# An attention and mixture-of-experts kernel: PSUM tiles in a named ring, value loads on SyncE's queue

## The chip, the cores and the metric

The kernel runs on one core of a Trainium2 chip. A core has TensorE (PE; its weight loads are listed as PEld), VectorE (DVE), ScalarE (ACT), GpSimd (POOL) and SyncE (SP), and 16 DMA engines that serve the transfers which SP, ACT and POOL issue. The metric is the device time of one execution in microseconds, median of several runs.

## The reference

Attention over 4 batches of 12 heads, 448 positions and head size 64, with the scores capped by `cap * tanh(scores / cap)`; its output, 1792 rows of 768, goes through a mixture of 8 experts, of which each row takes the one with the highest gate logit:

```python
scores = cap * np.tanh(scale * np.matmul(q, k.transpose(0, 1, 3, 2)) / cap)
attn = np.exp(scores - np.max(scores, axis=-1, keepdims=True))
attn = attn / (np.sum(attn, axis=-1, keepdims=True) + 1e-09)
x = np.matmul(attn, v)                                  # (4, 12, 448, 64) -> (1792, 768)
e_idx = np.argmax(x @ w_gate, axis=1)
h = np.maximum(x[mask] @ w1[e], 0.0)                    # for each expert e, mask = e_idx == e
out[mask] = gate_w[mask, None] * eom[mask, e, None] * (h @ w2[e])
```

`gate_w` is the softmax weight of the chosen expert, `eom` a sigmoid of `x @ w_output_gate`. Inputs and output are float32.

## The kernel before, in words

The work has two halves. In the attention half a loop (line 908) goes over 24 units; unit u is a pair of heads of one batch (six pairs per batch). The expert half takes the rows, sorted by expert, through `w1` and `w2` in blocks; its matmuls (line 1006) read weights that ACT and DVE have split into a high and a low part.

One turn of the loop for unit u does, in the order in which each engine gets its instructions:

- PE makes three score tiles `s` (`qk`, line 344; each holds both heads for 128 keys) and a fourth, half as large (`s3`, line 349). ACT takes the tanh of each out of PSUM into `pt` (line 351), then the exponential of the whole of `pt` in one instruction (line 353). `pt` has two buffers.
- PE multiplies unit u-1's `pt` with its values into `u` (`pv`, line 361, 16 matmuls), which ACT or DVE copies to `ut` (`u_evac`, lines 380 and 382).
- DVE turns K and Q of unit u+2 (`t_k`, `t_q`: a transpose at line 294 into `tk`, then a high and a low part). POOL adds up `pt` over keys (`presum`, lines 370 to 375), which PE sums across partitions every second unit (line 394).
- `slot` calls (line 897) put in the work that ends the batch before: PE turns `ut` into rows (`trow`, line 535), DVE scales them (`xr`, line 539) and SP's queue writes them to `xs` (line 544); gate products (`tg`, line 441; `pg`, line 456), ranks (`trk`) and POOL's table writes (line 526) belong to it too. In the last batch but one these steps also choose the experts' blocks, and the first weights are fetched.

The order on each engine is the order of the code. All score tiles, `u`, and the tiles `trow`, `tg`, `pg`, `trk` and `trec` of the batches' ends but the last's come from one pool, `ps_s`, of three PSUM buffers of two banks each (`scores` and `half`, lines 316 and 319). A tile can be written when the tile that had its buffer before has been read. Which of the three free buffers a tile gets is the pool's choice while the program is built, and is fixed in the program.

DMAs: K (`load_k`, six per unit into `kk`, four buffers) and Q (`load_q`, four for two units, `lq`) are issued on SP's queue, four units ahead of the loop, after the first scores; the values (`load_v`, four per unit, `vv`, three buffers) on ACT's queue right behind the exponential, for the next unit. The `xs` writes stand on SP's queue too. A queue issues its DMAs in its order. Each DMA of SP and ACT gets one of eight completion counters (DMAHW0 to DMAHW7), which go round over both queues, and is issued only when the DMA that had the counter before it has landed.

Of the kernel before, what the change touches and what calls it, by code (L numbers as in the profile page):

```python
# [9 lines left out]
F32 = mybir.dt.float32  # L10
# [12 lines left out]
def tile_kernel(ctx: ExitStack, tc, q, k, v, cap, w_gate, w_ogate, w1, w2, out):  # L23
    nc = tc.nc
# [46 lines left out]
    utp = rou.enter_context(tc.tile_pool(name="utp", bufs=8, side="right"))  # L71
    xrp = rou.enter_context(tc.tile_pool(name="xrp", bufs=3, side="right"))
    rtp = rou.enter_context(tc.tile_pool(name="rtp", bufs=1, side="right"))
# [6 lines left out]
    ptp = att.enter_context(tc.tile_pool(name="ptp", bufs=2))  # L80
    ps_s = att.enter_context(tc.tile_pool(name="ps_s", bufs=3, space=PSUM))

# [228 lines left out]
    def turn_next(n):  # L311
        for f, u in turns[:n]:
            f(u)
        del turns[:n]

    def scores(name):
        return ps_s.tile([128, 2, 512], F32, tag="s", name=name)

# [3 lines left out]
    def prep_first():  # L322
        pk = tbank([128, SK + 128], "tk0")
        for c in range(NK + 1):
            nc.tensor.transpose(pk[:, c * 128:(c + 1) * 128], k0[:, c].rearrange("p j d -> p (j d)"), ident)
        pq = ps_s.tile([128, 2, 512], F32, tag="s", name="tq0")[:, 0, 0:S]
        for c in range(NCH):
            nc.tensor.transpose(pq[:, c * CP:(c + 1) * CP], q0[:, c].rearrange("p j d -> p (j d)"), ident[0:CP, 0:CP])
        pl[0] = planes_of(0, pk, "K", SK + 128) + planes_of(0, pq, "Q", S)
        scales()  # L330
# [67 lines left out]
    rt = {}  # L398
    moe = []
    sh = [CP, NCH, E]  # L400

# [4 lines left out]
    def end_of_batch(b):  # L406
# [130 lines left out]
        def row_out(p):  # L537
            x = xrp.tile([CP, NCH, 128], F32, tag="xr", name="xr")
            nc.vector.tensor_tensor(  # L539
                out=x.rearrange("p c (j d) -> p c j d", j=2), in0=rt["trow"].rearrange("p c (j d) -> p c j d", j=2),  # L540
                in1=rec[b][:, :, 2 * p:2 * p + 2].unsqueeze(3).to_broadcast([CP, NCH, 2, D]), op=ALU.mult)
            for j in range(2):
                h = p + j * NP
                (nc.gpsimd if b == B - 1 else nc.sync).dma_start(
                    out=xs[b * S:(b + 1) * S, D * h:D * h + D].rearrange("(c p) m -> p c m", c=NCH),
                    in_=x[:, :, D * j:D * j + D])
# [361 lines left out]
    for u in range(NU):  # L908
# [11 lines left out]
        qk(u, NK)  # L920
        load_v(u + 1, nc.scalar)
        slot(u, "h")
# [360 lines left out]
```

## Time and profile before

| | us |
|---|---|
| median of 3 runs | 575.87 (574.64 to 578.27) |
| profiled execution | 577.18 |
| its span, first to last instruction | 575.3 |
| PE busy | 514.5 |
| ACT busy | 373.3 |
| DVE busy | 371.7 |
| POOL busy | 304.6 |

The profile is of one execution; times in it count from the first instruction. Busy time is an average over halves with different limits, so each stage is read by itself. An entry such as "0.97 <-PE s L344" says that the engine stood idle for 0.97 us before the instruction, and that PE's work on `s` at line 344 ended the wait. The granted clock is the share of 2.4 GHz that PE was given.

### The profile page before, as it was taken

The page shows a single profiled execution, that of the slowest core. Times are in us where ns is not written, and L with a number is a line of the kernel's source. Part 1 is how long each engine was busy: PE and PEld are TensorE (multiplying, and loading weights), DVE is VectorE, ACT ScalarE, POOL GpSimd, SP SyncE. Part 2 cuts the span into 40 slices and gives each one's busy share as a digit, 9 for nine tenths or more (in the row PEclk, how much of TensorE's full clock was granted, in tenths as well). Part 3 has the DMA queues.
Part 4 walks back from the last instruction along what each step waited for, and adds up shares of the span by engine and source line. Part 5 has one row for each costly group of instructions (what it writes and reads, how often), then busy time and mean ns, then how long its engine had stood idle before and what let it go on. Part 6 is the DMA issues. An engine that isn't in the chain of part 4 may idle for free. (4 is left out here: it accounts for less than half of the span.)

```text
span 575.3 us, 10035 instructions
## 1 busy us (share of the span) xinstructions
PE 514.5 (89%) x3053; PEld 348.9 (61%) x3053; DVE 371.7 (65%) x629; ACT 373.3 (65%) x425; POOL 304.6 (53%) x347
## 2 busy tenths in 40 slices
PE   7798678987678788896999999999999999999994
PEld 5444333533333245433789899789788886767692
DVE  4545656574254577776999998697576775646460
ACT  6688646777545657565375898687677776656561
POOL 8868744764954476644570576731474804362001
PEclk9799978999877997798999999999999999999998
DMA  6655443554551645368860992442956968985001
GB/s 144 95 88 92 74 72 64 93 92 84 58 89 28 117 81 93 65 169 287 277 228 1 339 398 67 159 152 85 380 202 214 389 268 338 411 281 238 8 29 45
DMA packets 157772, 91.93 MB, mean 160 GB/s; under 512 B 140418, under 2 KB 140554, under 8 KB 157712
## 3 DMA queue, kind: packets, MB, share of 16 engines
q1 hardware_dynamic: 125632, 52.96, 35.1%
q0 software_dynamic: 8832, 32.74, 15.2%
q10 hardware_dynamic: 23248, 5.53, 4.6%
q8 instruction: 26, 0.43, 0.3%
q14 instruction: 34, 0.28, 0.2%
HBM read 123.68 MB, written 12.04 MB: 236 GB/s over the span
## 5 line engine op out<-in xcount | busy, mean ns | idle before, releaser
L985 DVE TENSOR_TENSOR wr<-raw,wr 128x768 fp32r<-128x768 f32 (+1 forms) x167 | 171.6, 1068 | 66.2 <-ACT wr L984 64.0
L984 ACT ACTIVATE wr<-raw 128x768 fp32r<-128x768 f32 (+1 forms) x167 | 150.4, 936 | 33.2 <-DMA raw<-in_moe_w_dram 13.0
L351 ACT ACTIVATE pt<-s,icap 128x896 f32<-128x896 f32 x96 | 84.6, 912 | 71.2 <-PE s L344 31.1
L361 PE MATMUL u<-pt,vv 128*64 128x448 f32 x384 | 88.0, 606 | 9.4 <-ACT pt L351 9.3
L1006 PE MATMUL py<-wr,hh 128*128 128x384 f32 x352 | 77.3, 340 | 0.0
L370 POOL TENSOR_TENSOR pa<-pt 128x896 f32<-128x896 f32 x22 | 46.1, 2095 | 57.4 <-ACT pt L353 48.8
L1006 PE MATMUL php<-wr,xh 128*128 128x512 f32 x264 | 74.7, 404 | 0.0
L353 ACT ACTIVATE pt<-pt,capc 128x3136 f32<-128x3136 f32 x24 | 69.8, 2910 | 0.8
L1075 POOL DMA_INDIRECT out_dram<-yo,ti x13 | 20.6, 1585 | 84.6 <-ACT yo L1073 61.1
L361 PEld LDWEIGHTS u<-pt,vv 128*64 128x64 f32 x384 | 28.3, 153 | 60.8 <-issue 41.7
L1006 PEld LDWEIGHTS py<-wr,hh 128*128 128x128 f32 x352 | 61.2, 188 | 4.0 <-issue 3.7
L1006 PEld LDWEIGHTS php<-wr,xh 128*128 128x128 f32 x264 | 47.5, 188 | 12.2 <-issue 2.1
L344 PE MATMUL s<-QH,KH 64*128 64x448 f32 x144 | 32.8, 450 | 23.9 <-ACT pt L351 16.8
L375 POOL TENSOR_TENSOR pb<-pb,pt 64x448 f32<-64x448 f32 x44 | 49.9, 1135 | 3.4
L371 POOL TENSOR_TENSOR pb<-pa,pt 128x896 f32<-128x896 f32 x22 | 46.2, 2099 | 4.4 <-PE sm L394 2.8
L294 DVE STREAM_TRANSPOSE tk<-kk 128x512 f32<-128x512 f32 x23 | 16.7, 725 | 47.2 <-DMA kk<-in_k_dram 45.4
L1006 PE MATMUL py<-wr,hl 128*128 128x384 f32 x176 | 44.8, 335 | 0.0
L344 PEld LDWEIGHTS s<-QH,KH 64*128 64x128 f32 x144 | 14.6, 197 | 47.3 <-ACT pt L351 23.9
L1006 PE MATMUL php<-wr,xl 128*128 128x512 f32 x132 | 41.5, 395 | 0.0
L1122 POOL DMA_DIRECT2D rh<-in_moe_w_dram x42 | 23.2, 555 | 23.0 <-DVE wr L985 13.6
L1006 PEld LDWEIGHTS py<-wr,hl 128*128 128x128 f32 x176 | 31.8, 188 | 0.0
L539 DVE TENSOR_TENSOR xr<-trow,rec 112x512 f32<-112x512 f32 x24 | 16.2, 687 | 20.9 <-DMA xs<-xr 10.7
(247 smaller groups left out, 828.5 us busy)
## 6 DMA issues: line engine op xcount, KB each, us to landing
raw<-in_moe_w_dram SPq DMA_DIRECT2D x78, 512.0 KB
raw<-in_moe_w_dram SPq DMA_DIRECT2D x104, 384.0 KB
rh<-in_moe_w_dram POOLq DMA_DIRECT2D x18, 512.0 KB
rh<-in_moe_w_dram POOLq DMA_DIRECT2D x24, 384.0 KB
lq<-in_q_dram SPq DMA_DIRECT2D x44, 112.0 KB
vv<-in_v_dram ACTq DMA_DIRECT2D x46, 96.0 KB
xs<-xr SPq DMA_DIRECT2D x36, 112.0 KB
kk<-in_k_dram SPq DMA_DIRECT2D x46, 56.0 KB
```

Source lines behind the costliest of these rows:

```text
L344: nc.tensor.matmul(ps[:, j, 0:S], lhsT=x[h, sl], rhs=y[h], start=(i == 0), stop=(i == 2))
L351: nc.scalar.activation(out=pt[u][:, 2 * s:2 * s + n], in_=ps, func=ACTF.Tanh, scale=icap)
L353: nc.scalar.activation(out=pt[u], in_=pt[u], func=ACTF.Exp, scale=capc)
L361: nc.tensor.matmul(ups[u][64 * j:64 * j + 64], lhsT=V[:, c, j, :], rhs=P[:, 2 * c + (j if c < NK else 0)], start=(c == 0), stop=(c == NK))
L370: eng.tensor_tensor(out=a, in0=P[:, 0:2], in1=P[:, 2:4], op=ALU.add)
L371: eng.tensor_tensor(out=s1[u], in0=a, in1=P[:, 4:6], op=ALU.add)
L375: eng.tensor_tensor(out=s1[u][h, j], in0=s1[u][h, j], in1=P[h, 2 * NK], op=ALU.add)
L984: nc.scalar.activation(out=t[:, 0, 0:F], in_=raw, func=ACTF.Copy)
L985: nc.vector.tensor_tensor(out=t[:, 1, 0:F], in0=raw, in1=t[:, 0, 0:F].bitcast(F32), op=ALU.subtract)
L1006: nc.tensor.matmul(ps[g][:, 0:n], lhsT=st[:, c], rhs=w[:, z, g * n:(g + 1) * n], start=(c == 0 and st is hi and z == 0), stop=(c == (KD, K ...
L1075: nc.gpsimd.indirect_dma_start(out=out, out_offset=bass.IndirectOffsetOnAxis(ap=ti, axis=0), in_=y, in_offset=None, bounds_check=NT - 1, o ...
L1122: nc.gpsimd.dma_start(out=d, in_=rows_of(src, e, w, c), **kw)
```

## The change

Three edits. `scores` takes its buffers by name, `s0`, `s1`, `s2`, in strict turn, each name with one buffer; the three buffers stay three. The row buffers `xr` get names in the same way. `load_v` is called with SP's queue in place of ACT's, at the same place in the code (the first call, before the loop, was on SP already).

```diff
--- before.py
+++ after.py
@@ -69,7 +69,7 @@
     wp1 = ctx.enter_context(tc.tile_pool(name="wp1", bufs=1))
     rou = ExitStack()
     utp = rou.enter_context(tc.tile_pool(name="utp", bufs=8, side="right"))
-    xrp = rou.enter_context(tc.tile_pool(name="xrp", bufs=3, side="right"))
+    xrp = rou.enter_context(tc.tile_pool(name="xrp", bufs=1, side="right"))
     rtp = rou.enter_context(tc.tile_pool(name="rtp", bufs=1, side="right"))
     smp = rou.enter_context(tc.tile_pool(name="smp", bufs=2, side="right"))
     ps_t = ctx.enter_context(tc.tile_pool(name="ps_t", bufs=1, space=PSUM))
@@ -78,7 +78,7 @@
     plp = att.enter_context(tc.tile_pool(name="plp", bufs=3))
     ldp = att.enter_context(tc.tile_pool(name="ldp", bufs=2))
     ptp = att.enter_context(tc.tile_pool(name="ptp", bufs=2))
-    ps_s = att.enter_context(tc.tile_pool(name="ps_s", bufs=3, space=PSUM))
+    ps_s = att.enter_context(tc.tile_pool(name="ps_s", bufs=1, space=PSUM))
 
     tpools = [ps_t]
 
@@ -313,8 +313,11 @@
             f(u)
         del turns[:n]
 
+    ring = [0]
+
     def scores(name):
-        return ps_s.tile([128, 2, 512], F32, tag="s", name=name)
+        ring[0] += 1
+        return ps_s.tile([128, 2, 512], F32, tag=f"s{ring[0] % 3}", name=name)
 
     def half(name):
         return scores(name)[:, 0]
@@ -323,7 +326,7 @@
         pk = tbank([128, SK + 128], "tk0")
         for c in range(NK + 1):
             nc.tensor.transpose(pk[:, c * 128:(c + 1) * 128], k0[:, c].rearrange("p j d -> p (j d)"), ident)
-        pq = ps_s.tile([128, 2, 512], F32, tag="s", name="tq0")[:, 0, 0:S]
+        pq = scores("tq0")[:, 0, 0:S]
         for c in range(NCH):
             nc.tensor.transpose(pq[:, c * CP:(c + 1) * CP], q0[:, c].rearrange("p j d -> p (j d)"), ident[0:CP, 0:CP])
         pl[0] = planes_of(0, pk, "K", SK + 128) + planes_of(0, pq, "Q", S)
@@ -397,6 +400,7 @@
 
     rt = {}
     moe = []
+    nrow = [0]
     sh = [CP, NCH, E]
 
     def T(nm, shape=None, dt=F32):
@@ -535,7 +539,8 @@
                 nc.tensor.transpose(ps[:, c, :], ut[b * NP + p][:, c * CP:(c + 1) * CP], ident)
 
         def row_out(p):
-            x = xrp.tile([CP, NCH, 128], F32, tag="xr", name="xr")
+            nrow[0] += 1
+            x = xrp.tile([CP, NCH, 128], F32, tag=f"xr{nrow[0] % 3}", name="xr")
             nc.vector.tensor_tensor(
                 out=x.rearrange("p c (j d) -> p c j d", j=2), in0=rt["trow"].rearrange("p c (j d) -> p c j d", j=2),
                 in1=rec[b][:, :, 2 * p:2 * p + 2].unsqueeze(3).to_broadcast([CP, NCH, 2, D]), op=ALU.mult)
@@ -918,7 +923,7 @@
         slot(u, "f")
         slot(u, "g")
         qk(u, NK)
-        load_v(u + 1, nc.scalar)
+        load_v(u + 1, nc.sync)
         slot(u, "h")
         if u > 0:
             for c in range(NK + 1):
```

No instruction of PE, DVE or POOL moves. What each engine waits for changes with the buffers. The buffers in the two built programs (A, B, C in the order of their addresses), for some turns of the loop; the line stands between what comes before the fourth score tile's products with `u` and what comes after:

```
turn   before                          changed
 7     sB sB sB s3B | uB tgA           sA sB sC s3A | uB tgC
 8     sC sC sC trecC s3A | uB         sA sB sC trecA s3B | uC
11     sB sA sC trowB trowA s3C | uC   sC sA sB trowC trowA s3B | uC
12     sC sB sC trkA trowB s3C | uC tgA   sA sB sC trkA trowB s3C | uA tgB
16     sA sA sA pgA pgB s3C | uC       sB sC sA pgB pgC s3A | uB
18     sB sB sB trkC trowA s3B | uB tgB   sA sB sC trkA trowB s3C | uA tgB
```

From turn 7 to the end of the loop the pool hands out 120 tiles; 30 of them get the buffer of the tile just before them in the program before, none in the changed one. The `xr` tiles go round their three addresses in turn in both.

ACT's queue, turns 3 and 4 of the loop: in the program before the value loads stand behind the exponential, each behind a counter.

```order
L351 ACTIVATE pt<-s_594,icap 128x448 [waits PE_49]
L353 ACTIVATE pt<-pt,capc 128x3136 [waits Activation_49]
L118 DMA vv_127<-in_v_dram 128x3x64 [waits DMAHW3_49,DMAHW0_49]
L118 DMA vv_127<-in_v_dram 128x3x64 [waits DMAHW4_49]
L122 DMA vv_127<-in_v_dram 64x64 [waits DMAHW5_49]
L122 DMA vv_127<-in_v_dram 64x64 [waits DMAHW6_49]
L351 ACTIVATE pt<-s,icap 128x896 [waits PE_49,Pool_49]
```

In the changed program they are gone, and the next unit's tanh follows.

```order
L354 ACTIVATE pt<-s_594,icap 128x448 [waits PE_49]
L356 ACTIVATE pt<-pt,capc 128x3136 [waits Activation_49]
L354 ACTIVATE pt<-s,icap 128x896 [waits PE_49,Pool_49]
L354 ACTIVATE pt<-s,icap 128x896 [waits PE_49] x2
L354 ACTIVATE pt<-s_680,icap 128x448 [waits PE_49]
```

SP's queue, turn 9, the end of its K load (six DMAs into one buffer of `kk`), the rows' writes and the start of turn 10's K load, before:

```order
L132 DMA kk_123<-in_k_dram 32x2x32 [waits DMAHW7_49]
L132 DMA kk_123<-in_k_dram 32x2x32 [waits DMAHW0_49]
L544 DMA xs<-xr 112x4x64 [waits DMAHW1_49,DVE_49]
L544 DMA xs<-xr 112x4x64 [waits DMAHW4_49]
L544 DMA xs<-xr 112x4x64 [waits DMAHW6_49,DVE_49]
L544 DMA xs<-xr 112x4x64 [waits DMAHW0_49]
L132 DMA kk_124<-in_k_dram 32x14x32 [waits DMAHW1_49]
```

and in the changed program, where the values of unit 10 stand between them, each behind PE's last read of its buffer as well:

```order
L132 DMA kk_123<-in_k_dram 32x2x32 [waits DMAHW7_49]
L132 DMA kk_123<-in_k_dram 32x2x32 [waits DMAHW0_49]
L549 DMA xs<-xr 112x4x64 [waits DMAHW1_49,DVE_49]
L549 DMA xs<-xr 112x4x64 [waits DMAHW2_49]
L549 DMA xs<-xr 112x4x64 [waits DMAHW3_49,DVE_49]
L549 DMA xs<-xr 112x4x64 [waits DMAHW4_49]
L118 DMA vv_127<-in_v_dram 128x3x64 [waits DMAHW5_49,PE_49]
L118 DMA vv_127<-in_v_dram 128x3x64 [waits DMAHW6_49,PE_49]
L122 DMA vv_127<-in_v_dram 64x64 [waits DMAHW7_49,PE_49]
L122 DMA vv_127<-in_v_dram 64x64 [waits DMAHW0_49,PE_49]
L132 DMA kk_124<-in_k_dram 32x14x32 [waits DMAHW1_49]
```

The counters of SP's DMAs now go round over SP's DMAs alone while the loop runs.

## Rows read from the trace of the kernel before

**Rows 1.** The page: span, busy time by engine, PE in 40 slices.
```profile
span 575.3 us, 10035 instructions
...
PE 514.5 (89%) x3053; PEld 348.9 (61%) x3053; DVE 371.7 (65%) x629; ACT 373.3 (65%) x425; POOL 304.6 (53%) x347
...
PE   7798678987678788896999999999999999999994
```

**Rows 2.** Busy us (xcount) of each engine by stretch, granted clock, DMA share, GB/s.
```profile
11.20:59.90 48.70, 40.72 (x226) 21.12 (x228) 26.96 (x43) 38.43 (x33) 39.53 (x55) 0.89 0.57 98
59.90:253.80 193.90, 155.70 (x851) 74.23 (x849) 113.51 (x244) 118.96 (x108) 117.21 (x81) 0.89 0.46 79
```

**Rows 3.** PE's waits, 59.9 to 253.8 us: total, times, longest.
```profile
PE s L344 <- ACT pt L351: 14.6, 15, 1.7
PE u L361 <- ACT pt L351: 8.9, 13, 0.7
PE trow L535 <- ACT pt L351: 5.7, 6, 3.6
PE s L349 <- ACT pt L351: 3.7, 7, 1.1
```

**Rows 4.** Order of time (start us, us, instruction, idle before), ACT, unit 16.
```profile
166.73 1.01 ACT L351 ACTIVATE pt<-s,icap 128x896 f32<-128x896 f32 x1 [0.97 <-PE s L344]
```

**Rows 5.** The same, ACT, unit 12: scores' tanh, exponential, copy of u.
```profile
129.63 2.99 ACT L351 ACTIVATE pt<-s,icap 128x896 f32<-128x896 f32 x3 [1.19 <-PE s L344]
133.59 0.63 ACT L351 ACTIVATE pt<-s,icap 128x448 f32<-128x448 f32 x1 [0.97 <-PE s L349]
134.25 2.91 ACT L353 ACTIVATE pt<-pt,capc 128x3136 f32<-128x3136 f32 x1
...
137.57 0.54 ACT L380 ACTIVATE ut<-u 128x448 f32<-128x448 f32 x1 [0.41 <-PE u L361]
```

**Rows 6.** The same, PE, unit 12: first two score tiles, u, sums.
```profile
128.65 0.48 PE L344 MATMUL s<-QH,KH 64*128 64x448 f32 x2
...
129.36 0.38 PE L344 MATMUL s<-QH,KH 64*128 64x448 f32 x2
...
134.27 3.23 PE L361 MATMUL u<-pt,vv 128*64 128x448 f32 x16 [0.72 <-ACT pt L351]
137.43 0.96 PE L394 MATMUL sm<-pb,ohc 128*32 128x448 f32 x8
```

**Rows 7.** POOL by line, 59.9 to 253.8 us: busy, mean ns, idle before.
```profile
L375 POOL TENSOR_TENSOR pb<-pb,pt 64x448 f32<-64x448 f32 x34 | 38.5, 1134 | 2.6
L371 POOL TENSOR_TENSOR pb<-pa,pt 128x896 f32<-128x896 f32 x16 | 33.5, 2097 | 3.9 <-PE sm L394 2.8
L370 POOL TENSOR_TENSOR pa<-pt 128x896 f32<-128x896 f32 x16 | 33.5, 2093 | 49.9 <-ACT pt L353 41.3 <-PE u L361 5.3 <-ACT den L510 3.0
L526 POOL DMA_INDIRECT tab<-ent,posi x12 | 11.7, 971 | 16.0 <-issue 9.1 <-DVE bkey L583 4.4 <-DVE tk L294 2.2
```

**Rows 8.** Order of time, SP's DMA queue, 150 to 169 us.
```profile
151.67 10.24 SPq L132 DMA_DIRECT2D kk<-in_k_dram  x6
...
162.97 3.07 SPq L132 DMA_DIRECT2D kk<-in_k_dram  x6
166.08 2.19 SPq L132 DMA_DIRECT2D lq<-in_q_dram  x4
```

**Rows 9.** Order of time, 157 to 164 us: ACT's V issues, DVE's turn of K.
```profile
157.81 0.92 ACTq L118 DMA_DIRECT2D vv<-in_v_dram  x2
159.11 1.12 ACTq L122 DMA_DIRECT2D vv<-in_v_dram  x2
...
163.45 0.73 DVE L294 STREAM_TRANSPOSE tk<-kk 128x512 f32<-128x512 f32 x1 [12.03 <-DMA kk<-in_k_dram]
```

**Rows 10.** SP's queue waits, 11.2 to 253.8 us.
```profile
SPq L132 <- DMA vv<-in_v_dram: 77.4, 27, 9.3
SPq L544 <- DMA vv<-in_v_dram: 28.3, 4, 10.2
```

**Rows 11.** Order of time at the start: SP's first K, unit 2's exponential.
```profile
1.94 4.39 SPq L132 DMA_DIRECT2D kk<-in_k_dram  x6
...
30.03 2.91 ACT L353 ACTIVATE pt<-pt,capc 128x3136 f32<-128x3136 f32 x1
```

**Rows 12.** Order of time, POOL: the first gather of the experts' rows.
```profile
257.54 1.14 POOL L801 DMA_INDIRECT xg<-xs,ti  x1 [7.88 <-DMA xs<-xr]
```

## The prediction

> **What bounds the kernel now.** I read the page first, for the span and the tensor engine's share, then the busy time by stretch, then who waits for whom inside the stretch that is not full, and last the order of time of two single units and of the DMA queues. The span is 575.3 us [rows 1]; in the slices PE sits at nine tenths or more from about 275 us to the end, so the second half (the experts) is bound by matmuls and the change has nothing there. The first half is not full. From the exponential of unit 6 to that of unit 23, 17 units in 193.9 us or 11.4 each, PE is busy 155.70, ACT 118.96, POOL 117.21, DVE 113.51 [rows 2]. The mean granted clock there is 0.89 of 2.4 GHz, so PE's work at the full level would be about 155.7 x 0.89 = 139 us. Nothing in this stage fills its 193.9, and PE's 38.2 us of idle time have a name: scores waiting for ACT's tanh 14.6, `u` 8.9, `trow` 5.7, the fourth score tile 3.7, together 32.9 [rows 3]. Those are all waits for a PSUM buffer of the pool `ps_s`.
>
> Two units show how. In unit 16 all three score tiles sit in one buffer (the table in the section on the change): tanh, then matmuls, then tanh, with ACT idle 0.97 us between [rows 4]. In unit 12 the three tanh follow each other in 2.99 us [rows 5]. So one tile that gets the buffer of the tile just before it costs about 0.97 us.
>
> **The PSUM ring in turn.** No instruction is added on PE, ACT or DVE; only the buffers change. In the stage 30 of 120 tiles of the pool take the buffer of their forerunner; in the changed kernel none does. At 0.97 each that is 29 us [rows 4].
>
> The other way to the same term is to build the unit anew. ACT alone needs 2.99 (three tanh) + 0.66 (the fourth, to the start of the exponential) + 2.91 + 0.54 (`u`'s copy) = 7.1 [rows 5]. Eleven of the 17 units put two other tiles between the third score tile and the fourth. With three buffers in strict turn the fourth then always gets the third's, so it waits for the third tanh: the 0.97 us of idle time that unit 12 shows before its fourth tanh [rows 5] stay, and ACT comes to 8.1. On PE the path from that tanh's end is 0.05 + the fourth score tile 0.71 (as 128.65 to 129.36) + `u` 3.16 (134.27 to 137.43) + the next unit's first score tile up to its tanh 0.98 (128.65 to 129.63), 4.9 us after 2.99, or 7.9; every second unit has the row sums before it, 0.96 more, 8.85 [rows 5, 6]. So these units take 8.1 or 8.85, mean 8.5; the six others 7.1. 11 x 8.5 + 6 x 7.1 = 136. About seven units carry one more gate group, priced like the sums row, 0.96: 7 us, 143.
>
> What is late next: POOL and the rest. POOL's three steps per unit take 2.09 + 2.10 + 2 x 1.13 = 6.5; the three units with four table writes add 4 x 0.97 = 3.9 there [rows 7], 2 us over a unit of 8.5, and the tanh two units on waits for it since there are two `pt` buffers: 6 us, 149. `u` and the next score tile now get buffers that DVE frees (`xr` from `trow`), behind DVE's turns of K and Q; the trace of before has hardly such a wait, so it lies between 0 and the 32.9 us that are now spent on ACT's buffers. I take a third, 11 us, because DVE, with 113.5/17 = 6.7 us of work for a unit of 8.5, is mostly but not always free when `trow` is done. Stage 160, gain 193.9 - 160 = **34 us**. Ends: 55 (PE's 139, everything else covered) and 0.
>
> **The row buffers.** The three `xr` buffers are taken in turn already in the kernel before (their addresses in the built program go round in threes), so new names change nothing: 0.
>
> **The value loads.** Four issues per unit leave ACT's queue and go to SP's, behind the unit's K and Q loads and its `xs` writes. On ACT they lie beside the exponential (issued from 157.81, within its 2.91) [rows 9]: 0 saved. On SP they cost 0.92 + 1.12 = 2.0 us per unit. SP then has 14 issues per unit (6 K, 2 Q in the mean, 4 V, 2 `xs`), at 3.07/6 and 2.19/4 each [rows 8] some 0.52, so 7.3 us, under the 8.5 of a unit: 0 paid, and what covers it is the unit's length.
>
> What they take away is a lock. All these DMAs share eight counters in program order, and a DMA waits until the one before it on its counter has landed. K loads on SP waited 77.4 us for V loads, `xs` writes 28.3 [rows 10]. One is seen whole: six K loads take 10.24 us from 151.67 where six others take 3.07; they go on only after ACT issues V at 157.81 [rows 8, 9], and DVE, idle for 12.03 us, turns K at 163.45 [rows 9]. SP thus runs behind ACT instead of ahead. PE's waits name no K or Q in this stage [rows 3], so this was slack at 11.4 us a unit; at 8.5 it would not be. I count the move as cover for the 34 us and give it no gain of its own in the stage.
>
> A rule of the Trainium skill speaks against it: "DMA: Bandwidth & Descriptors", section "Issuing engines are not separate DMA queues", says that DMAs of all issuing engines run on the same 16 DMA engines, and that issuing from several saves the sequencer's time alone. By that rule the move can only cost, the 2.0 us of SP per unit; the sum by it is the same as long as 7.3 stays below 8.5, and the slower rival below is what it becomes where that fails. No row of before shows SP as the bound.
>
> **Start and end.** Units 0 to 6 take 48.7 us for six periods, 8.1 each, with ACT busy 38.43 [rows 2]: few repeats there, no routing. V of unit 1 now stands behind K and Q of units 1 to 5 on SP, the 43rd to 46th issue there, so it leaves at 24 to 34 us by 0.52 to 0.73 each (0.73 is the start's own rate, six in 4.39); it is read beside unit 2's exponential, now at 30.03 [rows 11]. What speaks the other way is that Q of unit 2 no longer waits for V's counters. I take -1 us, between -4 and +6. At the end, weights are fetched while units 21 to 23 run, and the first gather waits 7.88 us for `xs` [rows 12]; with shorter units less of it is hidden: +2, between 0 and +6.
>
> **Sum.** -34 - 1 + 2 = -33. The profiled execution took 577.18 us, 1.3 over the median 575.87 of the runs shown; 577.18 - 33 = 544, against the median **543 us**.
>
> **Rivals.**
> - *PE becomes the bound.* The ring lets PE run ahead, the clock rises to its upper level and stays, DVE and POOL hide. Stage 139: 577 - 55 - 1 + 2 = 523. For it: 32.9 of the 38.2 us of idle time are buffer waits. Against: the 0.97 before every fourth tanh stays in eleven units. Chance 0.15.
> - *DVE takes the place of ACT.* Strict turn forbids picking a free buffer, so `u` and the next score tiles wait for `xr`, and `xr` waits behind K. If half of 32.9 comes back so instead of a third, and the clock stays at 0.89 (155.7 of PE's time cannot be undercut, plus that 16): stage 172 to 176, gain 20, 558. For it: 12.03 us of DVE idle time in one wait. Chance 0.23.
> - *Nothing is left over.* The pool's choice was as good as the turn because routing on DVE sets the pace: within 1%, 576. Against: units with repeats show ACT idle before each tanh. Chance 0.05.
> - *Slower: SP becomes the bound.* Place: SP's queue, where K, Q, V and `xs` now stand in one line and an `xs` write that waits for DVE holds V and K behind it. It decides once a DMA costs 11.4/14 = 0.81 us on SP. At the start's 0.73 a unit is 10.2 long and the kernel still gains 20; at 0.9 it is 12.6, the stage 214, +20, 597. Against: 0.52 in rows 8 and DMA engines not full at 79 GB/s in the stage [rows 2]. Chance 0.05.
>
> **How the numbers follow.** Forecast 543 with chance 0.52, its own range 531 to 553. PE-bound 523 and DVE 558 are taken in, with the start's and end's ends: 519 to 563, which leaves out nearly the last two rivals and a little of each tail, under 2 in 10. One per cent, about what a measurement of this kernel can tell from no change, is 5.8 us. Faster: 0.52 + 0.15 + 0.23 = 0.90; same 0.05; slower 0.05.
>
> **What would show it.** Right: in the stage three tanh in some 3.0 us in every unit, none at 1.98; PE's waits for `pt` under 15 us; SP's waits for V gone from the top and no tk wait of many us on DVE; units near 9.4 or less; the expert half as long as before. Wrong: PE or ACT waiting for `xr` or `ut` of DVE (second rival); V late at `u` with SP busy without a gap (slower rival); a granted clock still at 0.89 with PE busy 155; or an expert half that starts earlier and then idles for weights.

## The result and the profile after

The changed kernel takes **536.78 us** (median of 4 runs, 534.74 to 537.59) against 575.25 for the kernel before on the same chip; the ratio is 0.9321, with a 95% interval of 0.927 to 0.9371. The profiled execution took 537.59 us, its span is 535.8. The forecast of 543 came out, and its main mechanism with it; how it shared the gain between the buffers and the value loads did not.

The page after. The first row counts busy time and its share of the span, the slices are fortieths of the span:

```profile
span 535.8 us, 10109 instructions
...
PE 496.4 (93%) x3053; PEld 344.8 (64%) x3053; DVE 378.7 (71%) x629; ACT 369.4 (69%) x425; POOL 303.1 (57%) x347
...
PE   7779999998989776799999999999999999999994
```

Against [rows 1], PE now stands at eight or nine tenths from the fourth slice on, but for four slices at six and seven, 174 to 228 us, where the attention half ends, and for the last. The same stretches as [rows 2], from the first exponential to that of unit 6 and from there to that of unit 23; columns as there:

```profile
11.60:59.90 48.30, 40.42 (x230) 21.31 (x232) 31.99 (x50) 37.40 (x33) 37.62 (x51) 0.89 0.63 106
59.90:215.10 155.20, 137.30 (x843) 69.19 (x841) 115.71 (x238) 116.01 (x108) 119.33 (x82) 0.97 0.56 99
```

The whole gain lies in the middle stretch: 193.9 us became 155.2, 38.7 less, while the exponential of unit 6 begins at 59.87 us (59.88 before) and from that of unit 23 to the end it takes 320.7 (321.5 before). The row also shows the clock. PE is busy 137.30 us instead of 155.70 with the same products, 18.4 less, at a granted clock of 0.97 instead of 0.89, and its idle time in the stage falls from 38.2 to 17.9, 20.3 less. The ratio of the two clocks alone would bring the busy time down to 142.9 us, an estimate; the 5.6 us beyond that are not explained (843 matmuls are recorded here, 851 before). No run holds the clock fixed, so how much of the gain it makes, and how much of it only follows from fewer waits, stays open.

PE's longest waits in that stretch (the releaser, us in total, times, longest), to be held against [rows 3]:

```profile
PE u L364 <- DVE xr L544: 6.6, 2, 5.3
PE trow L539 <- ACT pt L354: 5.4, 9, 1.7
PE s L352 <- ACT pt L354: 2.2, 9, 0.2
PE s L347 <- DVE ut L385: 1.7, 3, 0.6
```

The 14.6 us of score tiles that waited for the tanh ahead of them are gone. Two units on ACT, [rows 4, 5] after the change; a row is start, length, instruction, and in brackets the idle time ahead of it:

```profile
88.09 2.80 ACT L354 ACTIVATE pt<-s,icap 128x896 f32<-128x896 f32 x3 [0.92 <-PE s L347]
91.87 0.63 ACT L354 ACTIVATE pt<-s,icap 128x448 f32<-128x448 f32 x1 [0.97 <-PE s L352]
92.53 2.91 ACT L356 ACTIVATE pt<-pt,capc 128x3136 f32<-128x3136 f32 x1
95.35 0.52 ACT L383 ACTIVATE ut<-u 128x448 f32<-128x448 f32 x1
95.89 2.80 ACT L354 ACTIVATE pt<-s,icap 128x896 f32<-128x896 f32 x3
99.66 0.63 ACT L354 ACTIVATE pt<-s,icap 128x448 f32<-128x448 f32 x1 [0.96 <-PE s L352]
```

Three tanh run in a row, and the 0.97 us ahead of the fourth stays, as the fourth tile has the buffer of the third. The next exponential begins at 100.33, so the two units take 83.83 to 92.53 and 92.53 to 100.33: 8.70 and 7.80. All engines in these two units, columns as in [rows 2]:

```profile
83.83:92.53 8.70, 8.70 (x55) 4.43 (x53) 4.93 (x10) 6.78 (x6) 7.24 (x6) 1.00 0.62 114
92.53:100.33 7.80, 7.30 (x47) 3.95 (x45) 7.34 (x14) 6.78 (x7) 5.66 (x4) 1.00 0.66 109
```

At the upper level of the clock (1.00, which is 2.4 GHz) PE works 8.70 of the first unit's 8.70 us: there the bound of the first rival, PE, is reached. In the second ACT's work and the 0.96 us ahead of its fourth tanh fill the 7.80.

On SP's queue no wait for a value load is left; those at the top are now for routing:

```profile
SPq L788 <- DVE bsm L588: 6.0, 1, 6.0
SPq L549 <- DVE xr L544: 5.2, 2, 4.7
SPq L549 <- DVE pos L516: 5.1, 1, 5.1
```

Two waits are new. On PE's rows, `u` of unit 1 waits for its values, which now stand behind K and Q on SP, and `u` of unit 21 waits for a row tile's buffer:

```profile
29.96 5.45 PE L364 MATMUL u<-pt,vv 128*64 128x448 f32 x16 [5.34 <-DMA vv<-in_v_dram]
...
204.69 5.04 PE L364 MATMUL u<-pt,vv 128*64 128x448 f32 x16 [5.29 <-DVE xr L544]
```

DVE's rows say why the second: two `trow` tiles were written at 196.73 and 197.63 and hold two buffers of the ring until DVE, busy with the choice of the experts' blocks and then with K and Q, makes their `xr`:

```profile
199.85 0.73 DVE L294 STREAM_TRANSPOSE tk<-kk 128x512 f32<-128x512 f32 x1
...
203.41 0.62 DVE L290 TENSOR_TENSOR QL<-tk,QH 128x448 fp32r<-128x448 f32 x1
203.95 1.28 DVE L544 TENSOR_TENSOR xr<-trow,rec 112x512 f32<-112x512 f32 x2
```

### The profile page after: what moved, and what is told of

The parts are those of the page before. It is cut to its first block, busy times and chain, and to the rows that moved or that the text cites. A ratio compares the mean times of both kernels' runs of the same rounds, so it can differ in the third digit from the quotient of the medians.

```text
span 535.8 us, 10109 instructions
## 1 busy us (share of the span) xinstructions
PE 496.4 (93%) x3053; PEld 344.8 (64%) x3053; DVE 378.7 (71%) x629; ACT 369.4 (69%) x425; POOL 303.1 (57%) x347
## 5 line engine op out<-in xcount | busy, mean ns | idle before, releaser
L989 ACT ACTIVATE wr<-raw 128x768 fp32r<-128x768 f32 (+1 forms) x167 | 150.3, 936 | 32.8 <-DMA raw<-in_moe_w_dram 10.2
L354 ACT ACTIVATE pt<-s,icap 128x896 f32<-128x896 f32 x96 | 82.1, 913 | 47.6 <-PE s L347 30.9
L364 PE MATMUL u<-pt,vv 128*64 128x448 f32 x384 | 83.2, 578 | 12.5 <-DVE xr L544 6.6
L1080 POOL DMA_INDIRECT out_dram<-yo,ti x13 | 18.7, 1441 | 86.1 <-ACT yo L1078 62.2
L1127 POOL DMA_DIRECT2D rh<-in_moe_w_dram x42 | 23.2, 558 | 21.9 <-DVE wr L990 13.6
L347 PE MATMUL s<-QH,KH 64*128 64x448 f32 x144 | 29.7, 404 | 5.1 <-DVE QH L284 3.4
L1011 PEld LDWEIGHTS php<-wr,xl 128*128 128x128 f32 x132 | 24.7, 187 | 6.0
L1181 POOL DMA_INDIRECT out_dram<-yh,toh x6 | 6.1, 1019 | 37.9 <-DMA tc<-tab 9.7
```

Source lines behind the costliest of these rows:

```text
L347: nc.tensor.matmul(ps[:, j, 0:S], lhsT=x[h, sl], rhs=y[h], start=(i == 0), stop=(i == 2))
L354: nc.scalar.activation(out=pt[u][:, 2 * s:2 * s + n], in_=ps, func=ACTF.Tanh, scale=icap)
L364: nc.tensor.matmul(ups[u][64 * j:64 * j + 64], lhsT=V[:, c, j, :], rhs=P[:, 2 * c + (j if c < NK else 0)], start=(c == 0), stop=(c == NK))
L989: nc.scalar.activation(out=t[:, 0, 0:F], in_=raw, func=ACTF.Copy)
L1011: nc.tensor.matmul(ps[g][:, 0:n], lhsT=st[:, c], rhs=w[:, z, g * n:(g + 1) * n], start=(c == 0 and st is hi and z == 0), stop=(c == (KD, K ...
L1080: nc.gpsimd.indirect_dma_start(out=out, out_offset=bass.IndirectOffsetOnAxis(ap=ti, axis=0), in_=y, in_offset=None, bounds_check=NT - 1, o ...
```

## The experiments

The theory: a tile that takes the buffer of the tile just before it costs about 0.97 us, and the value loads on SP earn nothing by themselves but cover that gain, since on ACT's queue they hold K and Q back. The rivals: the move does the work; the ring's names are what counts, not the repeats; any second issuing engine costs the same. Each ratio below is to the kernel before on the same chip; between the chips the median of the kernel before goes from 575.0 to 577.3, so times of two runs are compared by their ratios. The table goes ahead, since the texts refer to it: the start of unit 6's exponential, from there to that of unit 23 (the stage), and from that to the end of the span, all of the profiled executions.

| kernel | median us | unit 6 | stage | end |
|---|---|---|---|---|
| before | 575.25 | 59.88 | 193.9 | 321.5 |
| after | 536.78 | 59.87 | 155.2 | 320.7 |
| after, once more | 536.24 | 59.13 | 154.8 | 320.2 |
| ring in turn, values on ACT | 551.26 | 60.52 | 170.7 | 317.5 |
| buffers of before, values on SP | 576.1 | 62.89 | 182.7 | 327.3 |
| pool's free choice, values on SP | 538.67 | 59.65 | 153.1 | 326.2 |
| every second tile repeats | 627.62 | 73.82 | 233.3 | 319.3 |
| ring, values on ACT, at the unit's front | 562.1 | 64.03 | 174.5 | 320.1 |
| ring, values on POOL | 568.67 | 63.99 | 177.2 | 325.6 |
| after, first values early | 538.91 | 58.28 | 157.1 | 320.6 |
| after, two rows later | 540.78 | 60.27 | 156.1 | 323.8 |
| after, last turns later | 540.63 | 59.56 | 154.5 | 324.2 |
| after, extras behind the fourth tile | 533.78 | 59.81 | 147.1 | 325.2 |
| that, rows ahead on SP | 531.58 | 58.80 | 149.8 | 319.4 |

**The ring alone.** The change without its last edit:

```diff
-        load_v(u + 1, nc.sync)
+        load_v(u + 1, nc.scalar)
```

> Only the ring in turn; the value loads stay on ACT's queue. My theory (the buffers are the gain, the value loads' move is its cover): part of the gain is lost again, because SP's K loads still wait behind ACT's V and at some 9 us a unit DVE's late turn of K reaches PE: 545 to 560, take 550; SP's waits for V stay at 80 us or more. Rival (the move of the loads is worth nothing, the ring is all): 537, within 3 of the changed kernel. Rival (the lock of the counters is all, the buffers nothing): 575.

551.26 us, ratio 0.9601 (0.9554 to 0.9647): the ring alone brings 24 us, and the move 14 on top. The lock is in the trace. SP waits for values nearly as it did before, 55.2 us in the stage where it was 60.8 there; over the whole loop it is 67.4 against the 77.4 of [rows 10], less than the 80 or more that were expected:

```profile
SPq L132 <- DMA vv<-in_v_dram: 55.2, 17, 7.8
```

Its queue shows one case: six K loads that are issued in 3.08 us in the second row take 8.39 in the first.

```profile
133.43 8.39 SPq L132 DMA_DIRECT2D kk<-in_k_dram  x6
...
142.88 3.08 SPq L132 DMA_DIRECT2D kk<-in_k_dram  x6
```

ACT issues the values that they wait for at 139.36, behind its exponential. DVE gets its K late, its `xr` stand behind the K turn, and PE's `u` behind these:

```profile
143.39 0.73 DVE L294 STREAM_TRANSPOSE tk<-kk 128x512 f32<-128x512 f32 x1 [11.56 <-DMA kk<-in_k_dram]
...
145.56 1.28 DVE L544 TENSOR_TENSOR xr<-trow,rec 112x512 f32<-112x512 f32 x2
```

```profile
146.29 5.22 PE L364 MATMUL u<-pt,vv 128*64 128x448 f32 x16 [7.64 <-DVE xr L544]
```

From this unit's exponential at 139.35 to the next at 157.75 it takes 18.4 us. With the buffers of before PE never named K or Q or `xr` [rows 3]; the slack that hid them is what the ring uses up.

**The move alone.** The ring's names, but by a table that gives every tile the buffer it had before, 30 repeats from turn 7 on:

```diff
+    TABLE = ("021021021021021020120101012121202020111110222201020201120120121021022212012202"
+             "121220221210120120000001222012011111201112020211021102102020201121021002120120")
-        return ps_s.tile([128, 2, 512], F32, tag=f"s{ring[0] % 3}", name=name)
+        return ps_s.tile([128, 2, 512], F32, tag=f"s{TABLE[ring[0] - 1]}", name=name)
```

> Every tile of the pool gets by name the buffer that it had in the kernel before (30 of 120 repeat their forerunner's from turn 7 on), and the value loads go on SP's queue. My theory: the tanh rows at 1.98 us stay in turns 7, 8, 16 and 18, the stage keeps most of its length: 565 to 572, take 568. Rival (the lock is the cause, repeats a symptom that hides behind it): about 540, with SP's waits for V gone. Rival (the move costs SP its issue time): 576 or more.

576.1 us, ratio 1.001 (0.9979 to 1.004): nothing, above the theory's bounds and at the number of the last rival, SP's issue time. DVE's waits for K are gone, and DVE waits for PE instead:

```profile
DVE gsb L284 <- PE tg L447: 23.7, 6, 9.8
DVE gm L469 <- PE pg L462: 13.5, 4, 9.1
```

PE still waits 14.0 us for the tanh ahead of a score tile. The table shows that nothing is a sum here: against the kernel before the stage is 11.2 us shorter, the start 3.0 longer (the values of unit 1 come late from SP's queue), the end 5.8 longer. So what the move loses it loses at the two ends, and not in the stage. Against the changed kernel, from which this run differs in the buffers alone, the stage is 27.5 us longer, 0.92 for each of the 30 repeats, and the two ends 9.6. At the end the first gathered rows come late to PE:

```profile
260.46 1.54 PE L820 MATMUL pt_x<-ident,xg 128*128 128x128 f32 x6 [6.94 <-DMA xg<-xs,ti]
```

In the kernel before that wait is 4.55 us, after the change 3.41.

**The pool's choice with the move.** Only the one line of `load_v` is changed; `ps_s` stays a pool of three.

```diff
-        load_v(u + 1, nc.scalar)
+        load_v(u + 1, nc.sync)
```

> Only the value loads go on SP's queue; the pool of three buffers chooses freely. With the loads there it chooses otherwise while the program is built: 3 repeats in place of 30. My theory (a repeat costs about 0.97 us, V on SP is the cover): 537 + 3 x 0.97 = 540, between 536 and 545. Rival (strict turn itself is needed, free choice makes other waits): 550 or more.

538.67 us, ratio 0.9372 (0.9333 to 0.9411), which overlaps that of the whole change. It does not contradict the run before: in the program built from this code the pool's choice repeats a buffer 3 times, not 30, each time for a `u` that takes the fourth score tile's. One line on a DMA's queue has moved PSUM buffers. The names make the good case certain; they are not the only way to it.

**More repeats.** Each name used twice running, 60 of the stage's 120 tiles repeat, 77 of 156 in all:

```diff
-        return ps_s.tile([128, 2, 512], F32, tag=f"s{ring[0] % 3}", name=name)
+        return ps_s.tile([128, 2, 512], F32, tag=f"s{ring[0] // 2 % 3}", name=name)
```

> The changed kernel, but every buffer name of the ring is used twice running, so that every second tile takes the buffer of the tile just before it: 60 of the stage's 120 tiles instead of none (before: 30). Theory (a repeat costs about 0.97 us of ACT's idle time, whatever else is as in the changed kernel): 537 + 60 x 0.97 = 595, up to 612 with the early units' repeats; ACT's wait for `s` in the stage about 50 to 60 us more than in the changed kernel. Rival (what the ring gives is that a tile waits for a known engine, not that it never waits for its forerunner): about 537, and below 550 in any case. Rival (DVE's routing sets the pace once V is out of the way): 545 to 560.

627.62 us, ratio 1.0877 (1.0831 to 1.0923). Repeats are the cause, and for these 0.97 is too small a price: the stage is 78.1 us longer for 60, 1.30 each, and the time is above the 612 that were expected at most. ACT's waits for score tiles in it, 19.7 and 11.0 us after the change, are 62.0 longer, a little over the 50 to 60 expected:

```profile
ACT pt L354 <- PE s L347: 47.7, 33, 5.1
ACT pt L354 <- PE s L352: 45.0, 16, 7.2
```

and the row of the stage shows how the clock went along:

```profile
73.80:307.10 233.30, 171.44 (x843) 80.28 (x843) 110.67 (x239) 118.67 (x108) 118.13 (x82) 0.82 0.35 65
```

The 843 recorded matmuls, as many as after the change, take 171.44 us at a granted clock of 0.82 where they took 137.30 at 0.97.

**Where the values are issued.** On ACT, but at the unit's front:

```diff
     for u in range(NU):
+        load_v(u + 1, nc.scalar)
         for s in range(NK):
...
-        load_v(u + 1, nc.sync)
```

> The ring in turn, and the value loads on ACT's queue as in the kernel before, but at the unit's front, ahead of its first tanh, and ahead of the K and Q loads in the program's order. Theory (what made the value loads cost 14 us with the ring in turn is not that ACT issues them but that K and Q on SP wait for completions of loads that ACT issues only after the fourth tanh): ACT now issues them some 5 us earlier in each unit, so SP waits less and DVE's waits for K go: 537 to 544. Rival (ACT's queue itself is the cost, four issues beside its tanh): 549 to 553, as with the value loads at their old place. Rival (any issue of ACT holds SP as long as it is in one order with K and Q): about 551 with SP's wait for V of the same size, 55 us.

562.1 us, ratio 0.976 (0.9719 to 0.9801). Every expectation missed: an earlier issue made it worse than at the old place, with 3.5 us more at the start, 3.8 in the stage and 2.6 at the end. SP still waits 59.8 us in its K loads for values. And ACT's own four issues now stand between the copy of `u` and the next tanh, where no exponential runs beside them:

```profile
93.66 0.91 ACTq L118 DMA_DIRECT2D vv<-in_v_dram  x2
94.62 1.16 ACTq L122 DMA_DIRECT2D vv<-in_v_dram  x2
95.89 2.80 ACT L354 ACTIVATE pt<-s,icap 128x896 f32<-128x896 f32 x3 [1.74 <-PE s L347]
...
142.14 1.25 ACTq L122 DMA_DIRECT2D vv<-in_v_dram  x2
145.65 2.81 ACT L354 ACTIVATE pt<-s,icap 128x896 f32<-128x896 f32 x3 [4.31 <-DMA vv<-in_v_dram]
```

The first score tile of that unit is begun at 94.35. From such a start to the tanh it was 0.98 us in [rows 5, 6], so the tanh could have begun at 95.33, an estimate; it begins 0.11 us behind the end of the last issue. Thirteen units of the stage begin in this way, and twelve of them are 0.5 to 1.4 us late by the same estimate, 8.8 us together. That is the cost which the first rival had put at the old place, where the issues lie beside the exponential.

The longest wait of ACT's that is put down to a value load, 4.31 us at 145.65, is another matter. The unit's first score tile was begun at 140.47 and ACT's last issue ended at 143.39; what ended at 145.61 is POOL's last addition out of the `pt` buffer that the tanh writes:

```profile
144.49 1.12 POOL L378 TENSOR_TENSOR pb<-pb,pt 64x448 f32<-64x448 f32 x1 [1.72 <-DMA tab<-ent,posi]
```

With the values on ACT at the old place the same unit's tanh, at 134.31, waits for POOL too. The theory was right that the counters couple the two queues, and wrong that an earlier issue frees SP.

On POOL, whose transfers have counters of their own:

```diff
-        load_v(u + 1, nc.sync)
+        load_v(u + 1, nc.gpsimd)
```

> The changed kernel with the value loads issued by POOL instead of SP, at the same place in the program. POOL's transfers have counters of their own (numbers 111 to 118 in the trace, SP's and ACT's share 100 to 109), so K and Q on SP share nothing with the value loads, though another engine issues these and late. Theory (what costs 14 us with ACT as issuer is the shared counters): SP's waits for V and DVE's long waits for K stay gone; paid is POOL's own time, four issues at about 0.7 us each, on an engine with 119 us of work in 155: 537 to 546. Rival (two engines issuing in one order is the cost, whatever the counters): about 551, as with ACT. Rival (POOL becomes the bound: 119 + 17 x 2.8 = 167 us in the stage): 549 to 552, then with ACT's waits for POOL's sums at the top, and no wait of SP or DVE for a load.

568.67 us, ratio 0.9867 (0.9842 to 0.9891). No wait for a load is among the longest of SP and DVE in the stage, as the theory has it: with counters apart, an engine that issues late does no harm to K and Q. The time is lost elsewhere, by the last rival's way: POOL is busy 167.0 of the stage's 177.2 us, the 167 that the rival had worked out, and in these rows it has no gap left and takes 9.3 us for a unit.

```profile
152.49 2.08 POOL L373 TENSOR_TENSOR pa<-pt 128x896 f32<-128x896 f32 x1
154.65 2.10 POOL L374 TENSOR_TENSOR pb<-pa,pt 128x896 f32<-128x896 f32 x1
156.82 2.35 POOL L378 TENSOR_TENSOR pb<-pb,pt 64x448 f32<-64x448 f32 x2
159.11 1.56 POOL L118 DMA_DIRECT2D vv<-in_v_dram  x2
160.67 1.07 POOL L122 DMA_DIRECT2D vv<-in_v_dram  x2
161.81 2.10 POOL L373 TENSOR_TENSOR pa<-pt 128x896 f32<-128x896 f32 x1
```

ACT's longest wait is then for POOL, which must read a `pt` buffer before it is written again: 28.0 us in the stage, 11 times. The units with POOL's table writes come on top (17 units at 9.3 are 158 of the 177.2), and so do, against the changed kernel, 4.1 us at the start and 4.9 at the end, which the rival did not have.

**The two new waits.** The values of unit 1 issued ahead of K of unit 3:

```diff
     load_q(2)
+    load_v(1, nc.sync)
     load_k(3)
...
-        load_v(u + 1, nc.sync)
+        if u > 0:
+            load_v(u + 1, nc.sync)
```

> The changed kernel, with the values of unit 1 issued before the K loads of unit 3, so that they land before unit 2's exponential. PE's wait of 5.3 us for vv at 24.6 to 30.0 us and ACT's 7.25 us behind it should go. My theory: SP is only late once, at the start, so 537 - 5 to 7 = 531, take 531. Rival (SP is late for what follows as well, K of units 3 and 4 then come late): 535 to 538, and PE waits for K or for unit 2's values instead.

538.91 us, ratio 0.9382 (0.9333 to 0.943): no gain. The 5.34 us are gone, and two smaller waits for values come instead:

```profile
34.99 4.78 PE L364 MATMUL u<-pt,vv 128*64 128x448 f32 x16 [0.42 <-DMA vv<-in_v_dram]
...
58.14 2.34 PE L364 MATMUL u<-pt,vv 128*64 128x448 f32 x10 [1.28 <-DMA vv<-in_v_dram]
```

The exponential of unit 6 begins 1.6 us earlier than after the change, that of unit 7 at 67.24 and not 67.33. In the first 60 us SP issues with hardly a gap, so what goes ahead makes something else late: up to 68 us DVE waits 6.3 us for K, where it waited 3.1 after the change. That is the rival, with a time a little above its range.

Unit 21's wait, in two ways, the rows later or the operand turns later:

```diff
-  (3, "g"): [rws[3], rws[4]], (3, "q"): [rws[5]],
+  (3, "g"): [rws[3]], (3, "q"): [rws[4], rws[5]],
```

> The changed kernel with the turn of rows 4 and 5 of the third batch (trow and xr) moved behind unit 21's `u` in unit 22, row 3 left ahead of it. Theory (in unit 22 `u` waits 5.29 us for an xr that stands behind the block choice and two operand turns on DVE, and the next tanh 8.20): `u` of unit 21 then only needs a buffer that ACT freed, so it starts at about 199 instead of 204.7 us; 537 - 4 to - 6, about 532. Rival (what waits only moves: the first score tile of unit 23 waits for xr or ut behind the same DVE work, or the experts' first gather waits that much longer for the rows in DRAM): 536 to 538.

```diff
-  NU - 4: (0, 2), NU - 3: (0, 2)}
+  NU - 4: (0, 2), NU - 3: (0, 0), NU - 2: (0, 2)}
```

> The changed kernel with the last two operand turns of DVE (K and Q of unit 23, 4.1 us) moved from behind the block choice in unit 21 to behind the two xr in unit 22. Theory: the two xr are made from 199.9 instead of 204.0 us, `u` starts 4 us earlier, and the operands of unit 23 are turned beside it: 537 - 3 to - 4, about 533. Rival (the scores of unit 23 then wait for the turned operands as long as `u` did for xr): 536 to 538.

540.78 us, ratio 0.9372 (0.9332 to 0.9413), and 540.63, ratio 0.9369 (0.9331 to 0.9406): no gain, rather a loss (the intervals overlap those of the changed kernel), and the second half of the first run's rival holds, at a time above its range. In both the experts' first gather comes later: POOL issues it at 220.07 and 219.76 us, 2.9 us behind the end of SP's last `xs` issue for the third batch (217.17, 216.84); after the change these are 217.09 and 214.20. With the turns moved the first two `xr` are made earlier, at 202.22, but their writes stand on SP behind eight table reads and go out at 210.91 only.

**A better order.** The rows and gate groups behind the fourth score tile:

```diff
-        slot(u, "g")
         qk(u, NK)
+        slot(u, "g")
```

> The changed kernel with the slot of the row tiles and gate groups moved behind the fourth score tile instead of ahead of it. In strict turn the fourth score tile then gets the buffer of the first, free long before, and `u` waits for the fourth tanh. Theory (in the eleven units with two such tiles ACT idles 0.97 us ahead of the fourth tanh, and it lies on the path): those waits, 11.0 us in the stage, go: 537 - 5 to - 10, about 530. Rival (the path runs from the third tanh over PE to the next unit's first score tile, and PE does the same work in it either way): 536 to 539, with the four tanh in one row and the wait in front of the next unit's first tanh instead.

533.78 us, ratio 0.9261 (0.9237 to 0.9286); the changed kernel beside it:

> The changed kernel itself once more, beside the two above on the same chip: 535 to 539.

536.24 us, ratio 0.9308 (0.9277 to 0.934). So this order is about 2.5 us faster, the intervals overlap by a little, and the gain is less than the 5 to 10 expected. Four tanh stand in a row, no 0.97,

```profile
88.36 3.33 ACT L354 ACTIVATE pt<-s,icap 128x896 f32<-128x896 f32 x4 [1.17 <-PE s L347]
91.73 2.92 ACT L356 ACTIVATE pt<-pt,capc 128x3136 f32<-128x3136 f32 x1
95.42 0.55 ACT L383 ACTIVATE ut<-u 128x448 f32<-128x448 f32 x1 [0.77 <-PE u L364]
96.26 3.33 ACT L354 ACTIVATE pt<-s,icap 128x896 f32<-128x896 f32 x4 [0.30 <-PE s L347]
```

but this pair of units takes 8.46 and 7.90 (exponentials at 83.27, 91.73 and 99.63), hardly less than 8.70 and 7.80, as the rival said: PE is busy 8.43 and 7.62 us of them, at a granted clock of 1.00. Of the 8.1 us by which the stage is shorter 7.1 lie in its last three units (179.60 to 206.87, after the change 180.67 to 215.08), where unit 21's wait does not arise. The end takes 4.5 us back:

```profile
220.96 1.54 PE L818 MATMUL pt_x<-ident,xg 128*128 128x128 f32 x6 [6.52 <-DMA xg<-xs,ti]
```

From this first matmul of the experts to the end of the span it is 311.1 us here, 311.1 after the change (224.68 to 535.8) and 310.8 before (264.49 to 575.3); over all the runs above it lies between 308.9 (ring in turn, values on ACT) and 315.6 (values on POOL). In these three kernels, then, what the attention half saves counts as far as it brings this matmul forward, and the matmul follows the last `xs` write. So the last version also takes the rows of the third batch ahead on SP:

```diff
-  (2, "e"): [fd[0], fd[1], P(set_known, NE), lds[0]], (3, "g"): [rws[3], rws[4]], (3, "q"): [rws[5]],
-  (3, "e"): [P(gather, 0), *lds[1:6], fd[2]], (4, "g"): [P(gather, 1), fd[3], *lds[6:]]}
+  (2, "e"): [fd[0], P(set_known, NE), lds[0]], (3, "g"): rws[3:6],
+  (3, "e"): [fd[1], P(gather, 0), *lds[1:6], fd[2]], (4, "g"): [P(gather, 1), fd[3], *lds[6:]]}
```

> The version with the rows and gate groups behind the fourth score tile (533.78), and on SP's queue the rows of the third batch ahead of what can wait: the second expert's table reads go behind them, and the last row is turned in the same place as the two before it, ahead of the value loads of unit 23. Theory (the end begins with the first gather, which POOL issues 2.9 us after the last `xs` write of that batch has been issued, 211.01 and 213.91 us in that version, 214.20 and 217.09 in the changed kernel; those writes stand behind eight table reads, 197.64 to 203.85, and four value loads, though their `xr` were made at 200 to 202): the last `xs` write goes out at 206 to 208, the first matmul of the experts 3 to 5 us earlier, and as it is 311 us from there to the end in every kernel, 529 to 531. Rival (the gather then waits for the tables, or for its own transfer, or unit 21's `u` for an xr more): 533 to 536.

**531.58 us**, ratio 0.9211 (0.9173 to 0.9249): faster than the changed kernel, with the intervals apart, and half a microsecond short of the expectation. Against the version above the intervals overlap by a little (0.9237 to 0.9249), so what the last edit adds by itself is not clear of noise. SP's queue has four table reads ahead of the rows now, not eight:

```profile
196.09 3.74 SPq L791 DMA_DIRECT2D tc<-tab  x4
...
201.09 3.90 SPq L549 DMA_DIRECT2D xs<-xr  x6
```

The gather goes out at 208.00, and the experts' first matmuls come in two parts:

```profile
214.73 0.65 PE L818 MATMUL pt_x<-ident,xg 128*128 128x128 f32 x4
217.85 0.44 PE L818 MATMUL pt_x<-ident,xg 128*128 128x128 f32 x2 [2.47 <-ACT ut L383]
```

The first four begin 6.2 us earlier than in the version above and wait for no gathered rows any more. The last two wait for ACT's copy of `u`, which stands on ACT behind two weight splits (215.00 and 216.31), and from them it is 310.2 us to the end. So the rows' way to DRAM has stopped being the bound there, and ACT's order is next. The rival is there too, at a smaller size: unit 21's `u` waits 3.07 us for an `xr` again.

## Why the prediction was right, step by step

- **The bound.** Shown: the score tiles' waits for a repeated buffer held the stage. Without the 30 repeats it is 27.5 us shorter with the values on SP in both kernels, and 23.2 with the values on ACT in both; with 60 repeats it is 78.1 longer than with none.
- **The price of a repeat.** 0.97 was read from ACT's gaps [rows 4], and for the 30 repeats of the program before it was near: 0.92 each with the values on SP, 0.77 with the values on ACT, where the late K takes the place of some of it. It is no constant of any repeat. The 60 of the run with every second tile cost 1.30 each, at a granted clock of 0.82; they are in part other tiles, 8 of them fourth score tiles and 7 `trow`, where the program before repeats 1 and 0. Strict turn also does away with 24 tiles of the stage that got the buffer of the tile two before them; no run has those without the repeats. The pool's free choice keeps 11 of them, and its stage is not longer for that (153.1 and 155.2).
- **The unit built anew.** Units of 8.1 and 8.85 were forecast, and 7.80 and 8.70 came. The difference lies on ACT: three tanh take 2.80 us in a row, not the 2.99 of [rows 5], and `u`'s copy begins 0.09 before the exponential ends. PE's part was priced right: `u` takes 3.23 us at a granted clock of 1.00 in unit 12 before and in the rows above. Not every unit is like these two. Units 20, 21 and 23 take 11.33, 10.74 and 14.98 us, the other fourteen 7.46 to 9.62.
- **POOL's 6 us.** Too much: ACT waits 1.1 us for POOL in the stage.
- **DVE's 11 us.** Near: 8.3 (6.6 for `xr`, 1.7 for `ut`), but 5.3 of it in one unit, behind the choice of blocks, not spread behind K and Q. PE waiting for `xr` or `ut` had been set down as a sign of the second rival; it came at half of that rival's 16.
- **The value loads as cover, no gain of their own.** It held in the total: alone they bring nothing, and without them the ring brings 24 instead of 38. In the stage, where the prediction put it, it did not hold: the move shortens the stage by 11.2 us alone and by 15.5 with the ring in turn (170.7 to 155.2), and the ring's own part is 23.2 to 27.5, not 34. Alone the move loses 8.8 us at the two ends, which hides its gain. That a part too large for the ring and none for the move add up to nearly the right stage, 160 and 155.2, is luck.
- **SP's load.** 7.3 us per unit were worked out. Between the value loads at 90.47 and the end of the `xs` writes at 106.19 two units' 28 issues stand in 15.7 us, 7.9 for a unit, so SP has little room at 7.80 and 8.70. Nothing waits for SP in the stage, and 0.56 us an issue is well under the 0.81 at which the slower rival was to decide.
- **The rule on issuing engines.** The Trainium skill, "DMA: Bandwidth & Descriptors", section "Issuing engines are not separate DMA queues", says that several issuing engines save sequencer time alone. Here SP's queue did take four more issues a unit, 2.1 us, and nothing waited for it in the stage; the inference drawn from the rule, that the move can only cost, fell with the ring in turn, where the move brings 14 us through the order of completions.
- **Start and end.** -1 and +2 were forecast, 0.0 and -0.8 came, and the zero is made of two parts. Unit 2's exponential begins 3.9 us earlier (26.15 and 30.03), unit 3's 2.8 later (39.68 and 36.93), behind the late values of unit 1 that were feared, 5.34 us. From there to unit 6 it takes 20.2 us after the change and 23.0 before, and 23.0 too with the buffers of before and the values on SP. No tile before turn 7 repeats its forerunner's buffer in the program before, but 13 have that of the tile two before; PE waits 2.2 us for the tanh there, and not at all after the change. So strict turn has a gain that the price of a repeat does not cover, and no run sets it apart.
- **The row buffers' names.** Not run apart. The run with the pool's free choice leaves them out, and its interval overlaps that of the whole change.

## What to carry to other kernels

Look at which buffer a tile gets, not only at how many there are: a pool that picks freely while the program is built can pick the buffer that was written last, and an unrelated edit can change its picks. A transfer that gains nothing today may be what a faster stage will wait for, so a move that measures as zero is tried again together with the edit that uses up its slack. And price a stage up to the first instruction of the next one that cannot come earlier by itself, here the experts' first gathered rows.

## What was not expected of the hardware

- The stage's matmuls were busy 136.6 us at a mean granted clock of 0.99 (extras behind the fourth tile), 137.30 at 0.97 (after), 141.75 at 0.92 (ring, values on ACT) and 171.44 at 0.82 (every second tile repeats). In these runs the clock went with PE's idle time in the stage, 10.5, 17.9, 29.0 and 61.9 us, and so it did before (38.2 at 0.89) and with the values on POOL (32.1 at 0.91). Others do not fit: 32.8 at 0.95 with the values on ACT at the unit's front, 35.4 at 0.93 with the buffers of before and the values on SP, 16.3 at 0.95 with two rows later. So the sum of idle time alone does not set it.
- What a wait takes besides itself: unit 21's `u` stands behind 5.29 us in which PE was idle. From its start at 204.69 to 207.00 the granted clock is 0.50, the lower level (1.2 GHz), and its 16 matmuls take 5.04 us; in the two units shown above, at 1.00, they take 3.23.
- A value load costs its issuing engine different times: the large one 0.78 us on POOL and 0.47 on SP (medians), the small one 0.54 on both.
- The stage moves the same amount with the values on ACT or on SP, some 15.4 MB by the rates of the two traces (90 GB/s in 170.7 us, 99 in 155.2), with the DMA engines busy 0.54 and 0.56 of the time. So the 14 us between the two are not a matter of how much is moved.
